# A transformer block on one Trainium2 core: layernorm tiles turned by DMA, and four smaller changes of order

## The chip, the cores and the metric

One core of a Trainium2 chip runs the whole kernel. The metric is the device time of one execution in microseconds (us). The engines are named as the profile names them: PE is TensorE's matrix products, PEld its weight loads, DVE is VectorE, ACT is ScalarE, POOL is GpSimd, and SP is SyncE, whose queue issues nearly all DMAs in program order.

## The reference

The input x has 2048 rows of 640 numbers in bf16. The block adds attention and then a gated product, each on a layernorm of what is there:

```python
x = A_x
h = x + _A_ref(_layernorm(x, axis=-1), A_wqkv, A_wo)      # 32 heads of 20, softmax over 2048 keys
h2 = h + _B_ref(_layernorm(h, axis=-1), B_w_gate, B_w_up, B_w_down)
# _B_ref: (x @ w_gate) * (x @ w_up) @ w_down, with 1728 inner columns
```

## The kernel before, in words

**Layout.** The 2048 rows are 16 tiles of 128, in four chunks of 512 (`QB`). Heads are packed four to a group (`HPG`), so there are eight groups (`NG`), each head in its slot of 32 partitions. Scores are made transposed (keys on partitions, 512 queries along the free side), so a *unit* is one tile of 128 keys by 512 scores of one head.

**The stream of units.** The exponentials are the body of the kernel. ACT takes most units, three or two banks at a time (line 727). DVE takes the rest with an integer trick: one operation per unit that writes int16 (line 739), and three per two units (lines 622, 624, 627). `on_dve` says how many units of a segment go to DVE (`D_CHUNK`, `D_WHOLE`, `D_HALF`), and those are the last ones of the segment's list, `units[cut:]`. Their due times lie between `EARLY` units before the segment's start and `LEAD` units before the end of ACT's part. PE makes the scores (line 719) and multiplies the exponentials with the values (line 857); the sums of the exponentials come out as an extra column.

**Segments and passes.** Pass 0 (the first 512 queries) goes chunk by chunk of keys for groups 0 to 3 (kinds "copy", "add", "last") and then whole for groups 4 to 7 (kind "only", 64 units each, 12 of them on DVE). Passes 1 to 3 are the other queries, partly cut in halves of 256.

**An order written out by a planner.** The Python code that builds the program keeps model clocks for PE, DVE and ACT (`clk`, `act_end`) and places every instruction by them. Each round `i` emits one exponential; the room left in the round, `limit_of`, with `EASE` or `HURRY` added, is filled with pieces of *jobs* from a queue: projections, transposes (`job_T`, `job_lnT`), output products, gated products. PE executes strictly in this order. If no job fits, `idle_products` adds products whose result is not used. `later(n, fn)` calls a function n rounds on.

**Layernorm.** DVE takes the statistics, POOL the inverse root, and DVE writes the normalized tile (`ln_apply`, line 240). For products over the 640 columns the tile must be turned: in `job_T` PE makes five transposes into a bank (line 320) and DVE copies them out (line 254). Layernorm 1 does this for four tiles per chunk into `lnT`; layernorm 2 does it in the tails, two tiles at a time, into `ln2T`. A turn may start 600 ns of model time after the tile is normalized (`ready`). The first four tiles (the head) and the last two (the end) are turned by code of their own.

**Keys and queries of most groups** go a longer way: a dense product (line 357), a copy to `dn`, a store to DRAM (line 365), and a read of it into the slots (line 388). The job's `READ` and `WRITE` are the model's times for this.

**Inverse sums.** When a segment closes, DVE copies its accumulator to SBUF (`asb_tile`; one wide buffer and two narrow). `norm` then sends the sums to DRAM and back (lines 757 and 758), POOL takes the inverse (line 761), it is stored (line 763) and read back spread over the partitions (line 766), and POOL multiplies (line 770). The two DMAs after POOL's inverse stand on SP's queue behind it.

**Tails.** When all groups of a set of rows are normalized, a tail is queued: output product with `wo`, residual, layernorm 2, turn, gated products (line 1174), down product (line 283) and store. The last tail (two tiles) comes after all units and has PE to itself. `wo` is loaded with four DMAs for each of eight groups (line 1039 clears the padding first); its tiles hold half of the query and key weights before that.

Of the kernel before, what the change touches and what calls it, by code (L numbers as in the profile page):

```python
# [18 lines left out]
P = 128  # L19
# [22 lines left out]
G1 = 4  # L42
GP = 4
D_CHUNK = (0, 0, 2, 2)
D_WHOLE = (12, 12, 12, 12)
D_HALF = (0, 6, 6, 6)
D_LAST = 4
SPLIT_1 = 4
# [19 lines left out]
SWITCH = 100  # L68
ROUND = 216
S_NS = SWITCH + ROUND  # L70
ACT_NS = {1: 478, 2: 904, 3: 1330}
RING = 2
EASE, HURRY = 100, 200
S_LAG = 270
AHEAD = 700
WAKE = 165
MINJOB = 600
AVLOW = 8
SLACK = 100
EB = (4, 3)  # L80
POOL_LN = 3500
WRITE, READ = 2500, 3500


@with_exitstack
def kernel(
# [39 lines left out]
    kb = const.tile([P, 1], F32, name="kb")  # L126
    qv = const.tile([P, 1], F32, name="qv")
    bad = const.tile([1, 1], I32, name="bad")
    wo = [const.tile([P, D], BF16, name=f"wo{g}") for g in range(NG)]
    NS = QB // SLOT  # L130
    seen_sums = const.tile([P, 2, NS], F32, name="seen_sums")

# [28 lines left out]
        nc.sync.dma_start(xs[0][:, t, :], x2d[t * P:(t + 1) * P, :])  # L161

    def wqk_half(c, hf):
        return (wo if hf else wqk)[c][:, 0:D].rearrange("p (m x) -> p m x", m=2)

    def load_wqk(hf):
        for c in range(KT):
# [157 lines left out]
        if given is None:  # L325
            ev(D // 2, held["slot"])

    def job_lnT(t):
        yield from job_T(lns[t], lnT[:, :, t * P:(t + 1) * P])

    def wslice(m, g, c):
        return wpad[c][:, m, HPG * g:HPG * (g + 1), :].rearrange("p h e -> p (h e)")
# [111 lines left out]
    for s, (p, g, lo, hi, _) in enumerate(segs):  # L444
        n = BANK // PASS[p][2]
        units = [(s, kt, j) for kt in range(lo, hi, n) for j in range(HPG)]
        cut = len(units) - on_dve(s)
        a0 = len(a_units)
        a_units += units[:cut]
        own = units[cut:]  # L450
        due += [a0 - EARLY + (cut - LEAD + EARLY) * (k + 0.5) / len(own) for k in range(len(own))]
        d_units += own
        left[s] = [n * (sum(u[2] == j for u in units) + sum(u[2] == j for u in own)) for j in range(HPG)]
# [296 lines left out]
    def norm(s, asb):  # L750
        p, g = segs[s][0:2]
        b, c0, w = PASS[p]
        n = w // 32
        rr = nrm.tile([P, 2, NS], F32, name="rr", bufs=3)
        r16, ri = rr[:, 0, 0:n], rr[:, 1, 0:n]
        sums = dram.tile([HPG, w], F32, name="sums", tag=f"sums{w}")
        nc.sync.dma_start(sums[:], asb[DH:P:SLOT, 0:w])
        nc.sync.dma_start(r16, sums[:].rearrange("j (c f) -> (j c) f", f=n))

        def back():  # L760
            nc.gpsimd.tensor_tensor(ri, r16, powers[:, 1:2].to_broadcast([P, n]), ALU.pow)  # L761
            scr = dram.tile([HPG, w], F32, name="scr", tag=f"scr{w}")
            nc.sync.dma_start(scr[:].rearrange("j (c f) -> (j c) f", f=n), ri)
            bc = nrm.tile([P, QB], F32, name="bc")
            for j in range(HPG):
                nc.sync.dma_start(bc[SLOT * j:SLOT * (j + 1), 0:w], scr[j:j + 1, :].to_broadcast([SLOT, w]))
            later(9, lambda: scale(bc))

        def scale(bc):
            nc.gpsimd.tensor_tensor(On[b % 2][g][:, c0:c0 + w], asb[:, 0:w], bc[:, 0:w], ALU.mult)  # L770
            note_sums(rr, n)
            later(4, lambda: done.add(("n", p, g)))
        later(8, back)

    def sums_to_rows(asb, w, ps=None):
        n = w // SLOT
        ps = bank() if ps is None else ps
        for t in range(w // P):
            nc.tensor.matmul(ps[:, HPG * t:HPG * (t + 1)], lhsT=asb[:, t * P:(t + 1) * P], rhs=late["if"][:, DH:P:SLOT], start=True, stop=True)
        mm(400, "turn")  # L780
        rr = nrm.tile([P, 2, NS], F32, name="rr", bufs=3)
        r16, ri = rr[:, 0, 0:n], rr[:, 1, 0:n]
        nc.vector.reciprocal(ri, ps[:, 0:n])
        bc = nrm.tile([P, QB], F32, name="bc")
        nc.vector.tensor_copy(bc[:, 0:w].rearrange("p (j e) -> p j e", e=SLOT), ri.rearrange("p (j e) -> p j e", e=1).to_broadcast([P, n, SLOT]))
        nc.vector.tensor_copy(r16, ps[:, 0:n])
        note_sums(rr, n)
        ev(w, held["slot"])
        return bc
# [72 lines left out]
            if sum(left[s]) == 0:  # L862
                close(s)

    sum_bufs = {"asb": -99, "ash0": -99, "ash1": -99}

    def asb_tile(w):
        tag = min(sum_bufs, key=lambda k: (sum_bufs[k], k)) if w == HW else "asb"
        sum_bufs[tag] = now["i"]
        return nrm.tile([P, QB if tag == "asb" else HW], F32, name=tag, bufs=1)  # L870

    def close(s):
        p, g, lo, hi, kind = segs[s]
        b, c0, w = PASS[p]
        if kind in ("copy", "only"):
            asb = parts[g] if kind == "copy" else asb_tile(w)
            if s == FINAL:
                nc.vector.tensor_copy(asb[:, 0:P], acc["t"][:, 0:P])
                nc.scalar.copy(asb[:, P:w], acc["t"][:, P:w])
            else:  # L880
                nc.vector.tensor_copy(asb[:, 0:w], acc["t"][:, 0:w])  # L881
            if kind == "copy":
                part[g] = asb
        else:
            asb = part[g]
            nc.vector.tensor_tensor(asb[:, 0:w], acc["t"][:, 0:w], asb[:, 0:w], ALU.add)
        dve_op(w / 0.96 + 75, clk["pe"] + 150)
        clk["acc"] = clk["dve"] + WAKE
        acc.update(seg=None, next=s + 1)
        acc["from"] = now["i"] + 2  # L890
        if s == FINAL:
            final["asb"] = asb
        elif (p, g) in FAST:
            urgent.append((("nf", p, g), job_norm(s, asb, clk["acc"]), None))
        elif kind in ("only", "last"):
            norm(s, asb)


# [62 lines left out]
    def gen_ln(ch):  # L961
        ts = range(ch * TPB, (ch + 1) * TPB)
        while hold(("x", ch)):
            yield WAIT
        mv = small.tile([P, TPB, 2], F32, name="mv")
        for k in range(TPB):
            bn(mv, k, xs[ch][:, k, :])
            yield 930
        for got in rstd_wait(mv, TPB):
            yield WAIT if got == WAIT else 0  # L970
        for k, t in enumerate(ts):
            apply1(t, *got, k)
            done.add(("a", t))
            ready["a", t] = max(clk["dve"], clk["pe"]) + 600
            yield 410

    def T_of(t):
        while hold(("a", t)):
            yield WAIT
        ensure_aux(("a", t))  # L980
        yield from job_lnT(t)

    def more_x(ch):
        load_x(ch)
# [50 lines left out]
    for t in range(NT):  # L1035
        value(t, 1)

    def load_wo(g):
        nc.gpsimd.memset(wo[g][:], 0.0)
        for j in range(HPG):  # L1040
            h = HPG * g + j
            nc.sync.dma_start(wo[g][SLOT * j:SLOT * j + DH, :], A_wo[DH * h:DH * h + DH, :])

    for b in range(1, NB):
        for t in range(KT):
            dense_job(0, t, b)
            if b == 1 and t + KT < NG:
                do(("wo", t + KT), lambda g=t + KT: load_wo(g))

    def spill(j):  # L1050
        src = dense[0][:, 0:QB].rearrange("(g j e) n -> j e g n", j=HPG, e=DH)
        nc.sync.dma_start(src[j, :, 0:G1, :], qa_all[SLOT * j:SLOT * j + DH, 0:G1, 0:QB])

    for g in range(KT):
        do(("wo", g), lambda g=g: load_wo(g))
        if g < HPG:
            do(("spill", g), lambda g=g: spill(g))


    late = {"res": {}}  # L1060
# [48 lines left out]
    def ln2_pieces(st, ts, key):  # L1109
        mv = small.tile([P, len(ts), 2], F32, name="mv")  # L1110
        for k, t in enumerate(ts):
            bn(mv, k, st["xr"][t][:])
            yield 930
        for got in rstd_wait(mv, len(ts)):
            yield WAIT if got == WAIT else 0
        for k, t in enumerate(ts):
            l_t = late["s"].tile([P, D], BF16, name="ln2")
            ln_apply(l_t[:], st["xr"][t][:], *got, k)
            st["l", t] = l_t
            done.add(("l2", key, t))  # L1120
            ready["l2", key, t] = max(clk["dve"], clk["pe"]) + 600
            yield 360

    def job_out(on, st, ts, key):
        pairs = [ts[k:k + 2] for k in range(0, len(ts), 2)]

        def T_pair(pair):
            for t in pair:
                while hold(("l2", key, t)) and end["pool"] is None and key is not None:
                    yield WAIT  # L1130
                ensure_aux(("l2", key, t))
                yield from job_T(st["l", t], st["ln2T"][:, :, t * P:(t + 1) * P])
        done.difference_update({("l2", key, t) for t in ts})
        while key is not None and hold(("xr",) + key):
            yield WAIT
# [252 lines left out]

    seen = {"t": 0, "last": False}
    i = 0  # L1390
    while pos["a"] < len(a_units) or pos["d"] < len(d_units):
        now["i"] = i
        emit_S(i)
# [37 lines left out]
    def general():  # L1431
        st = new_st(None)
        st["res"] = {}
        with tc.For_i(0, S, P) as r0:
# [1 line left out]
            load_tail(st, [0])  # L1436
            load_w(0, st)
            for g in range(NG):
                qs = nrm.tile([P, P], BF16, name="qs", tag="bc")
                nc.vector.memset(qs[:], BETA)  # L1440
                for j in range(HPG):
                    h = HPG * g + j
# [32 lines left out]
                ri = nrm.tile([P, HPG, 1], F32, name="ri", tag="rr", bufs=3)  # L1475
                ov = o[:, 0:P].rearrange("p (j e) -> p j e", e=SLOT)
                nc.vector.reciprocal(ri[:], ov[:, :, DH:VS])
                oq = nrm.tile([P, HPG, SLOT], BF16, name="oq", tag="asb", bufs=1)
                nc.vector.memset(oq[:], 0.0)
                nc.vector.tensor_tensor(oq[:, :, 0:DH], ov[:, :, 0:DH], ri[:].to_broadcast([P, HPG, DH]), ALU.mult)  # L1480
                ps = bank(BF16, P)
# [38 lines left out]
```

## Time and profile before

| | |
|---|---|
| median of three runs | 901.35 us (896.91 to 902.56) |
| the profiled execution | 899.62 us, span 897.8 us |
| PE, DVE, ACT, POOL busy | 92%, 78%, 90%, 22% of the span |
| granted PE clock, mean | 0.978 |
| DMA queue of SP | 95396 packets, 56.02 MB |

The profile page gives busy time by engine, the granted clock and the DMA share in 40 slices, the chain of work that ended last, and groups of instructions with the idle time before them. Other views of the same trace give single stretches, single tiles, and the order of instructions in time. A busy PE is not a PE at its peak, and idle time of an engine costs only where another waits for it.

### The profile page before, as it was taken

What the parts mean: (1) busy time and instruction counts of PE and PEld (TensorE: products, weight loads), DVE (VectorE), ACT (ScalarE), POOL (GpSimd) and SP (SyncE); (2) the same over time, 40 slices, a digit from 0 to 9 for tenths busy, and PEclk for the clock granted to TensorE, in tenths of its full rate; (3) what the DMA queues carried; (4) which work ended last, traced back from release to release, by engine and by line L of the source; (5) the groups of instructions that cost most, each with busy time, mean ns of one, the idle gap of its engine ahead of it and who ended that gap; (6) DMA issues with size and microseconds to landing.
All of it is one profiled execution on the core that took longest, in us unless ns stands there. A gap on an engine that the chain in (4) does not pass through costs nothing.

```text
span 897.8 us, 34224 instructions
## 1 busy us (share of the span) xinstructions
PE 830.1 (92%) x15185; PEld 406.0 (45%) x15185; DVE 704.3 (78%) x1384; ACT 804.0 (90%) x710; POOL 195.5 (22%) x258
## 2 busy tenths in 40 slices
PE   6899989998999999999899988999999999999996
PEld 4334333332334334445444545554553465445664
DVE  6665767996778989988888888988889888788631
ACT  6899997999999999999989999999999899999630
POOL 2110035123112321322312231223102412122100
PEclk8999999999999999999989999999999899899999
DMA  6111231342012232101314122322603010031310
GB/s 182 57 43 54 73 89 56 81 114 47 14 41 76 70 116 74 37 23 32 88 48 115 52 67 73 98 57 56 175 10 102 16 46 16 23 83 45 82 45 18
DMA packets 95550, 58.26 MB, mean 65 GB/s; under 512 B 24548, under 2 KB 93284, under 8 KB 95396
## 3 DMA queue, kind: packets, MB, share of 16 engines
q1 hardware_dynamic: 95396, 56.02, 23.1%
q8 instruction: 120, 1.97, 0.9%
q14 instruction: 34, 0.28, 0.1%
HBM read 47.60 MB, written 8.16 MB: 62 GB/s over the span
## 4 chain that ended last, share of the span: by engine, by line
PE 50%; DVE 23%; ACT 17%; issue 4%; DMA 3%; SPq 2%; POOL 0%; DVEq 0%; ACTq 0%; POOLq 0%
ACT E L727 17%; PE sc L719 12%; PE acc L857 10%; PE mi L1174 10%; PE mi L283 9%; DVE di L739 7%; DVE di L627 3%; DVE dm L622 2%; PE mi L357 2%; DVE dt L624 2%; PE f L1174 2%; DVE st L216 2%; PE f L283 1%; DVE hh L1206 1%; DVE u L254 1%
## 5 line engine op out<-in xcount | busy, mean ns | idle before, releaser
L727 ACT ACTIVATE E<-sc 128x1536 bf16<-128x1536 f32 (+1 forms) x679 | 786.7, 1263 | 43.9 <-PE mi L719 21.3
L739 DVE TENSOR_SCALAR di<-mi 128x512 int16<-128x512 f32 x350 | 238.0, 684 | 74.8 <-PE mi L719 71.6
L857 PE MATMUL acc<-E,vx 128*32 128x256 bf16 (+1 forms) x2532 | 224.4, 318 | 4.2 <-DVE asb L881 1.5
L719 PE MATMUL sc<-qa,kT 21*128 21x256 bf16 (+1 forms) x1800 | 206.2, 321 | 17.5 <-ACT E L727 14.4
L719 PEld LDWEIGHTS <-kT 21*128 21x128 bf16 x3072 | 85.6, 92 | 226.3 <-issue 215.1
L761 POOL TENSOR_TENSOR rr<-rr,powers 128x8 f32<-128x8 f32 (+1 forms) x44 | 98.7, 2243 | 304.7 <-DMA rr<-sums 291.8
L857 PEld LDWEIGHTS <-vx 128*32 128x32 bf16 x3612 | 82.3, 96 | 108.6 <-issue 98.2
L627 DVE TENSOR_TENSOR di<-di,dm 128x1024 bf16<-128x1024 bf16 x175 | 121.3, 693 | 4.1
L719 PE MATMUL mi<-qa,kT 21*128 21x256 bf16 (+1 forms) x376 | 99.0, 314 | 4.2 <-DMA kT<-dense 2.4
L622 DVE TENSOR_SCALAR dm<-di 128x1024 int16<-128x1024 int16 x175 | 79.7, 455 | 3.9
L857 PE MATMUL acc<-dt,vx 128*32 128x256 bf16 (+1 forms) x540 | 77.8, 313 | 2.8 <-DVE asb L881 2.0
L857 PE MATMUL acc<-di,vx 128*32 128x256 bf16 (+1 forms) x540 | 78.2, 313 | 0.7 <-DVE di L627 0.3
L624 DVE TENSOR_SCALAR dt<-di 128x1024 int16<-128x1024 int16 x175 | 77.8, 445 | 0.0
L719 PE MATMUL sc<-qb,kT 21*128 21x256 bf16 (+1 forms) x732 | 67.9, 294 | 4.7 <-ACT E L727 4.6
L283 PE MATMUL mi<-wd,hh 128*32 128x320 bf16 (+1 forms) x1432 | 67.2, 300 | 1.8 <-DVE hh L1206 0.7
L1174 PE MATMUL mi<-ln2T,wu 128*32 128x256 bf16 (+1 forms) x1210 | 58.8, 307 | 5.2 <-DVE di L739 2.5
L1174 PE MATMUL mi<-ln2T,wg 128*32 128x256 bf16 (+1 forms) x1210 | 54.7, 297 | 2.0 <-DVE di L739 0.8
L283 PEld LDWEIGHTS <-hh 128*32 128x32 bf16 (+1 forms) x1516 | 45.5, 96 | 20.3 <-issue 10.2
L1174 PEld LDWEIGHTS <-wu 128*32 128x32 bf16 (+1 forms) x1230 | 35.1, 99 | 19.9 <-issue 15.5
L283 PE MATMUL mi<-kT,ident 128*32 128x512 bf16 x608 | 43.2, 392 | 0.5 <-DVE dn L363 0.2
L1174 PEld LDWEIGHTS <-wg 128*32 128x32 bf16 (+1 forms) x1230 | 34.0, 96 | 13.6 <-issue 9.6
L1206 DVE TENSOR_TENSOR hh<-mi,u 128x512 bf16<-128x512 f32 (+1 forms) x48 | 31.7, 660 | 10.2 <-PE mi L1174 9.8
(135 smaller groups left out, 770.0 us busy)
## 6 DMA issues: line engine op xcount, KB each, us to landing
wu<-in_B_w_up_dram SPq DMA_DIRECT2D x30, 320.0 KB
wg<-in_B_w_gate_dram SPq DMA_DIRECT2D x30, 320.0 KB
dense<-dn SPq DMA_DIRECT2D x36, 128.0 KB
bc<-scr SPq DMA_DIRECT2D x64, 64.0 KB
bc<-scr SPq DMA_DIRECT2D x112, 32.0 KB
xr<-in_A_x_dram SPq DMA_DIRECT2D x16, 160.0 KB
out_dram<-xr SPq DMA_DIRECT2D x14, 160.0 KB
wd<-in_B_w_down_dram SPq DMA_DIRECT2D x13, 160.0 KB
```

Of the source, the lines that this page charges most:

```text
L216: nc.vector.bn_stats(st[:, h, :], halves[h] if halves else src[:, h * HALF:(h + 1) * HALF])
L283: nc.tensor.matmul(out[k:k + w, :], lhsT=lhsT[:, k:k + w], rhs=rhs, **flags)
L622: nc.vector.tensor_scalar(m16[:, 0:n], s16, M_MASK, M_BITS, ALU.bitwise_and, ALU.bitwise_or)
L624: nc.vector.tensor_scalar(t16[:, 0:n], s16, E_MASK, E_BITS, ALU.bitwise_and, ALU.bitwise_or)
L627: nc.vector.tensor_tensor(sb[:, 0:n], sb[:, 0:n], mb[:, 0:n], ALU.mult)
L719: nc.tensor.matmul(dst[:, h * w:(h + 1) * w], lhsT=kT[g][SLOT * j:SLOT * j + VS, (kt + h) * P:(kt + h + 1) * P], rhs=q_of(g, b, c0, w)[SLO ...
L727: nc.scalar.activation(e[:, 0:n], sc[:, 0:n], ACT.Exp, bias=EXP_BIAS, scale=SM_SCALE)
L739: nc.vector.tensor_scalar(t[:, k * BANK:(k + 1) * BANK], sd[:], EXP_A, 0.0, ALU.mult, ALU.max)
L761: nc.gpsimd.tensor_tensor(ri, r16, powers[:, 1:2].to_broadcast([P, n]), ALU.pow)
L857: nc.tensor.matmul(acc["t"][SLOT * j:SLOT * (j + 1), 0:w], lhsT=vx[kt][:, VS * h:VS * h + SLOT], rhs=e, start=(j not in acc["new"]), stop= ...
L1174: nc.tensor.matmul(ps[r0 + x:r0 + x + d, col:col + n], lhsT=wt[:, c, f0 + x:f0 + x + d], rhs=st["ln2T"][:, c, c0:c0 + n], start=(c == 0), ...
L1206: nc.vector.tensor_tensor(st["hh"][fp][:, f2:f2 + k, c0:c0 + n], g, u, ALU.mult)
```

## The change

- The turns of layernorm 1 for tiles 4 to 15, and of layernorm 2 for all tiles but the end's two, are five transposing DMAs each on SP, issued right after the tile is normalized (`turn`). Jobs may use the tile `TURN` = 6000 ns later by the model.
- In pass 0, groups 4 to 7, DVE takes the first keys of the segment instead of the last, and 14 units instead of 12.
- `norm` issues each hop in a later round than the one before it: read after 2, inverse after 4, store after 3, spreading read after 3, multiplication after 6. The "last" segments of groups 0 to 3 wait another `REST` + 6 g rounds first.
- Sums have two wide buffers and a narrow one, `bc` one wide and one narrow; the one that was taken longest ago is used.
- `wo` is one tile, cleared by POOL in spaced rounds and loaded with four DMAs.
- Model constants: `ACT_NS`, `EASE`, and DVE's clock at the start.

```diff
-D_WHOLE = (12, 12, 12, 12)
+D_WHOLE = (14, 12, 12, 12)
...
-ACT_NS = {1: 478, 2: 904, 3: 1330}
+ACT_NS = {1: 490, 2: 917, 3: 1343}
...
-EASE, HURRY = 100, 200
+EASE, HURRY = 50, 200
...
+REST = 30
...
+TURN = 6000
...
-    wo = [const.tile([P, D], BF16, name=f"wo{g}") for g in range(NG)]
+    wo_all = const.tile([P, NG, D], BF16, name="wo")
+    wo = [wo_all[:, g, :] for g in range(NG)]
...
-    def job_lnT(t):
-        yield from job_T(lns[t], lnT[:, :, t * P:(t + 1) * P])
+    def turn(dst, src, key):
+        for c in range(KT):
+            nc.sync.dma_start(dst[:, c, :], src[:, c * P:(c + 1) * P], transpose=True)
+        done.add(key)
+        ready[key] = max(clk["dve"], clk["pe"]) + TURN
...
         cut = len(units) - on_dve(s)
+        if p == "0" and g >= G1:
+            units = units[-cut:] + units[:-cut]
...
-        nc.sync.dma_start(r16, sums[:].rearrange("j (c f) -> (j c) f", f=n))
-
-        def back():
+
+        def read():
+            nc.sync.dma_start(r16, sums[:].rearrange("j (c f) -> (j c) f", f=n))
+            later(4, invert)
+
+        def invert():
             nc.gpsimd.tensor_tensor(ri, r16, powers[:, 1:2].to_broadcast([P, n]), ALU.pow)
+            later(3, write)
+
+        def write():
             scr = dram.tile([HPG, w], F32, name="scr", tag=f"scr{w}")
             nc.sync.dma_start(scr[:].rearrange("j (c f) -> (j c) f", f=n), ri)
-            bc = nrm.tile([P, QB], F32, name="bc")
+            later(3, lambda: spread(scr))
+
+        def spread(scr):
+            bc = bc_tile(w)
             for j in range(HPG):
                 nc.sync.dma_start(bc[SLOT * j:SLOT * (j + 1), 0:w], scr[j:j + 1, :].to_broadcast([SLOT, w]))
-            later(9, lambda: scale(bc))
+            later(6, lambda: scale(bc))
...
-        later(8, back)
+        later(2, read)
...
     def asb_tile(w):
-        tag = min(sum_bufs, key=lambda k: (sum_bufs[k], k)) if w == HW else "asb"
-        sum_bufs[tag] = now["i"]
-        return nrm.tile([P, QB if tag == "asb" else HW], F32, name=tag, bufs=1)
+        return oldest({"asb0": QB, "asb1": QB, "asb2": HW}, w)
+
+    def bc_tile(w):
+        return oldest({"bc0": QB, "bc1": HW}, w)
...
-        elif kind in ("only", "last"):
+        elif kind == "last":
+            later(REST + g * 6, lambda: norm(s, asb))
+        elif kind == "only":
             norm(s, asb)
...
             apply1(t, *got, k)
-            done.add(("a", t))
-            ready["a", t] = max(clk["dve"], clk["pe"]) + 600
+            turn(lnT[:, :, t * P:(t + 1) * P], lns[t], ("a", t))
...
         ensure_aux(("a", t))
-        yield from job_lnT(t)
...
+            for j in range(HPG):
+                nc.sync.dma_start(wo_all[SLOT * j:SLOT * j + DH, :, :], src[j])
...
             st["l", t] = l_t
-            done.add(("l2", key, t))
-            ready["l2", key, t] = max(clk["dve"], clk["pe"]) + 600
+            turn(st["ln2T"][:, :, t * P:(t + 1) * P], l_t, ("l2", key, t))
...
                 ensure_aux(("l2", key, t))
-                yield from job_T(st["l", t], st["ln2T"][:, :, t * P:(t + 1) * P])
...
     i = 0
+    clk["dve"] = max(clk["dve"], clk["pe"])
```

More of the change, by code (lines that the diff above doesn't have):

```diff
@@ L163, in wqk_half @@
     def wqk_half(c, hf):
-        return (wo if hf else wqk)[c][:, 0:D].rearrange("p (m x) -> p m x", m=2)
+        return (wo[c] if hf else wqk[c][:]).rearrange("p (m x) -> p m x", m=2)
     def load_wqk(hf):
@@ L783, in sums_to_rows @@
         nc.vector.reciprocal(ri, ps[:, 0:n])
-        bc = nrm.tile([P, QB], F32, name="bc")
+        bc = bc_tile(w)
         nc.vector.tensor_copy(bc[:, 0:w].rearrange("p (j e) -> p j e", e=SLOT), ri.rearrange("p (j e) -> p j e", e=1).to_broadcast([P, n, SLOT]))
@@ L863, in emit_AV, with oldest @@
                 close(s)
-    sum_bufs = {"asb": -99, "ash0": -99, "ash1": -99}
+    used_at = {}
+    def oldest(tags, w):
+        tag = min((k for k, n in tags.items() if n >= w), key=lambda k: (used_at.get(k, -99), k))
+        used_at[tag] = now["i"]
+        return nrm.tile([P, tags[tag]], F32, name=tag, bufs=1)
     def asb_tile(w):
-        tag = min(sum_bufs, key=lambda k: (sum_bufs[k], k)) if w == HW else "asb"
-        sum_bufs[tag] = now["i"]
-        return nrm.tile([P, QB if tag == "asb" else HW], F32, name=tag, bufs=1)
+        return oldest({"asb0": QB, "asb1": QB, "asb2": HW}, w)
+    def bc_tile(w):
+        return oldest({"bc0": QB, "bc1": HW}, w)
     def close(s):
@@ L1036, with clear_wo, load_wo, read @@
         value(t, 1)
[L1038 to L1042, printed above, removed]
+    def clear_wo(g):
+        nc.gpsimd.memset(wo[g], 0.0)
+    def load_wo():
+        for g in range(KT):
+            later(2 * g + 1, lambda g=g: clear_wo(g))
+        def read():
+            src = A_wo.rearrange("(g j e) n -> j e g n", j=HPG, e=DH)
+            for j in range(HPG):
+                nc.sync.dma_start(wo_all[SLOT * j:SLOT * j + DH, :, :], src[j])
+        later(2 * KT + 2, read)
+    for g in range(KT, NG):
+        later(9 * g, lambda g=g: clear_wo(g))
     for b in range(1, NB):
@@ L1046 @@
             dense_job(0, t, b)
-            if b == 1 and t + KT < NG:
-                do(("wo", t + KT), lambda g=t + KT: load_wo(g))
     def spill(j):
@@ L1052, in spill @@
         nc.sync.dma_start(src[j, :, 0:G1, :], qa_all[SLOT * j:SLOT * j + DH, 0:G1, 0:QB])
[L1054 to L1057, printed above, removed]
+    do(("wo",), load_wo)
+    for j in range(HPG):
+        do(("spill", j), lambda j=j: spill(j))
     late = {"res": {}}
@@ L1438, in general @@
             for g in range(NG):
-                qs = nrm.tile([P, P], BF16, name="qs", tag="bc")
+                qs = nrm.tile([P, P], BF16, name="qs", tag="bc0", bufs=1)
                 nc.vector.memset(qs[:], BETA)
@@ L1477, in general @@
                 nc.vector.reciprocal(ri[:], ov[:, :, DH:VS])
-                oq = nrm.tile([P, HPG, SLOT], BF16, name="oq", tag="asb", bufs=1)
+                oq = nrm.tile([P, HPG, SLOT], BF16, name="oq", tag="asb0", bufs=1)
                 nc.vector.memset(oq[:], 0.0)
```

## The prediction, written before the changed kernel ran

> **What bounds the kernel now.** I read the page first, then the stages, then the places where ScalarE (ACT) stops.
>
> ```profile
> span 897.8 us, 34224 instructions
> PE 830.1 (92%) x15185; PEld 406.0 (45%) x15185; DVE 704.3 (78%) x1384; ACT 804.0 (90%) x710; POOL 195.5 (22%) x258
> ```
> ```profile
> 28.00:125.00 97.00, 92.99 (x1339) 36.03 (x1340) 67.35 (x134) 94.43 (x84) 8.42 (x11) 1.00 0.20 60
> 125.00:150.00 25.00, 21.29 (x368) 9.55 (x360) 16.53 (x32) 18.17 (x16) 15.55 (x12) 0.93 0.20 55
> 150.00:270.00 120.00, 112.41 (x1421) 36.44 (x1417) 94.82 (x174) 116.69 (x103) 25.89 (x22) 0.99 0.24 61
> 270.00:846.00 576.00, 543.45 (x11439) 281.53 (x11439) 490.98 (x945) 547.78 (x472) 137.88 (x149) 0.98 0.25 65
> 846.00:898.00 52.00, 40.59 (x423) 30.92 (x411) 16.02 (x45) 9.16 (x18) 0.22 (x1) 0.94 0.10 28
> ```
> The columns of the second view are the stretch, its length, busy time of PE, PEld, DVE, ACT, POOL, then the granted clock. Until 846 us ACT's exponentials are the bound: ACT is busy 94.43 of 97 us, then 116.69 of 120, then 547.78 of 576. PE is nearly as full (543.45), but part of that is idle products which the scheduler puts in. The last 52 us are PE's own chain. So time is won before 846 us only by taking exponentials off ACT or by closing its gaps: 6.83 us in 125 to 150 and 28.22 us in 270 to 846; and at the end by giving PE less left-over work.
>
> ```profile
> 64.09 2.13 ACT E L727 x2
> ...
> 75.27 2.25 ACT E L727 x2
> ```
> In the chain that ended last, five pairs (3 + 2 units of 512 columns) lie between these two rows: 11.18 us for 25 units, so one unit is 0.447 us of a full ACT.
>
> ```profile
> 133.61 1.45 ACT L727 ACTIVATE E<-sc 128x1536 bf16<-128x1536 f32 x1 [2.13 <-PE sc L719]
> 135.74 1.02 ACT L727 ACTIVATE E<-sc 128x1024 bf16<-128x1024 f32 x1 [0.68 <-PE mi L719]
> 137.20 2.36 ACT L727 ACTIVATE E<-sc 128x1536 bf16<-128x1536 f32 x2 [0.44 <-PE sc L719]
> 146.97 3.33 ACT L727 ACTIVATE E<-sc 128x1024 bf16<-128x1024 f32 x3 [3.34 <-PE mi L719]
> ```
> ```profile
> 127.06 1.72 SPq L766 DMA_DIRECT2D bc<-scr  x4
> 128.82 1.52 SPq L388 DMA_DIRECT2D kT<-dense  x4
> 132.52 0.39 PE L719 MATMUL mi<-qa,kT 21*128 21x512 bf16 x1 [2.45 <-DMA kT<-dense]
> 143.22 2.35 PE mi L283 x60
> ```
> These are ACT's idle times in the worst stretch and what stands behind them. PE waited 2.45 us for the keys of the last chunk, which the read at L388 brings. It sat on SyncE's (SP's) queue behind the inverse-sum hop at L766. The waiter is a `mi` product: a DVE unit, and DVE's units of that segment were the *last* keys. That one wait gave ACT 2.13 + 0.68 + 0.44 = 3.25 us of idle, 1.33 us for each of PE's. The second gap, 3.34 us, stands behind a burst of value projections (L283 x60).
>
> **The change, part by part.** The sum is made against the profiled execution: 899.6 us, of which 897.8 are its span; the three runs have a median of 901.35, 1.7 above it.
>
> *First keys to DVE, the last norms put off.* From the fifth head group of pass 0 on, DVE takes keys 0 to 3 and ACT starts at the fourth, so chunk 3 is needed some 34 ACT units (34 x 0.447 = 15 us) later, and REST moves the four "last" norms 30 to 48 rounds back, out of SP's way. The first gap (3.25) goes; the second shrinks if PE is ahead by the turns it no longer makes (below). Bounds: 3 us if the burst stays, 6.8 if ACT gets full. I take **-6**, nearer to the upper end, because the stretches beside it have ACT at 97%.
>
> *14 units instead of 12 to DVE in four segments.* Eight units leave ACT: 8 x 0.447 = 3.6 us. What DVE gets:
>
> ```profile
> L739 DVE TENSOR_SCALAR di<-mi 128x512 int16<-128x512 f32 x350 | 238.0, 684 | 74.8 <-PE mi L719 71.6
> L627 DVE TENSOR_TENSOR di<-di,dm 128x1024 bf16<-128x1024 bf16 x175 | 121.3, 693 | 4.1
> L622 DVE TENSOR_SCALAR dm<-di 128x1024 int16<-128x1024 int16 x175 | 79.7, 455 | 3.9
> L624 DVE TENSOR_SCALAR dt<-di 128x1024 int16<-128x1024 int16 x175 | 77.8, 445 | 0.0
> ```
> A unit is 0.684 + (0.693 + 0.455 + 0.445)/2 = 1.48 us, eight are 11.8. DVE has 25 us idle in 150 to 270, so they are covered; without that cover a late unit holds a bank and PE behind it, and the 3.6 could turn into +2. I take **-3**.
>
> *Three sum buffers for one wide and two narrow.*
>
> ```profile
> DVE asb L881 <- POOL on L770: 2.4, 1, 2.4
> 200.00:250.00 50.00, 45.82 (x561) 14.76 (x558) 36.42 (x66) 47.95 (x44) 11.91 (x7) 0.97 0.15 36
> ```
> The one wide buffer made DVE, and PE behind it, wait 2.4 us for POOL; ACT lost 2.05 us in that stretch, which includes the usual. Two wide buffers end this. **-1.5** (0 to -2).
>
> *The turns.* 26 tiles (12 in layernorm 1, 14 in layernorm 2) no longer take five PE transposes, a DVE copy and two switches each; the head's four and the end's two stay.
>
> ```profile
> L320 PE MATMUL mi<-ident,ln 128*128 128x128 bf16 x70 | 6.9, 238 | 2.1 <-DVE di L739 1.7 <-DVE ln2T L254 0.2
> 448.00:458.00 10.00, 8.74 (x93) 3.69 (x92) 7.83 (x17) 7.13 (x7) 2.86 (x4) 0.67 0.07 16
> 538.00:546.00 8.00, 5.73 (x129) 3.71 (x127) 6.57 (x16) 6.43 (x7) 2.06 (x3) 1.00 0.07 19
> 622.00:630.00 8.00, 7.74 (x184) 4.58 (x180) 7.51 (x17) 7.96 (x8) 3.78 (x4) 1.00 0.11 21
> 709.00:718.00 9.00, 8.11 (x120) 3.99 (x119) 7.85 (x16) 5.96 (x6) 2.88 (x3) 0.62 0.02 3
> 807.00:815.00 8.00, 7.04 (x162) 4.16 (x158) 7.30 (x16) 7.48 (x8) 3.38 (x4) 1.00 0.08 15
> ```
> The PE time itself (about 0.5 us a tile) lies beside a busy ACT and is worth little. The waits around it are worth more: PE waits in order for the normalized tile, then for its copy. In the five stretches around a tail's turn ACT is idle 43 - 34.96 = 8.04 us; at the rate of the rest of 270 to 846 (20.2 us in 533) it would be 1.6. In two of the five the granted clock is 0.67 and 0.62. So up to 6.4 us lie there. With DMAs that are on time PE comes to the tile when it has long been turned. **-4.5** (0 to -6.4). Layernorm 1's turns fall where ACT is full, and are worth nothing but PE's lead into 125 to 150, counted above.
>
> *What the 130 new DMAs cost.* The trace has none of this kind. The nearest rows for an SP issue:
>
> ```profile
> 139.84 0.34 SPq L758 DMA_DIRECT2D rr<-sums  x1
> 12.98 4.12 SPq L196 DMA_DIRECT2D kT<-di  x7
> 811.89 2.99 SPq L766 DMA_DIRECT2D bc<-scr  x4
> 837.08 2.19 SPq L1091 DMA_DIRECT2D xr<-in_A_x_dram  x2
> ```
> That is 0.34, 0.59, 0.75 and 1.10 us for one. Call it d. From the last issue to the use took 132.52 - 130.34 = 2.2 us. A pair of tiles is ten DMAs and the schedule lets PE come about 6.4 us after the first tile is normalized (0.4 for the second, TURN 6.0): late by 10 d + 2.2 - 6.4, so on time up to d = 0.42. A 32 KB block in the queue's plain form is nearest to the 0.34 row; I take d = 0.4 and **0**. At the other end (1.1) each of seven pairs is 6.8 us late. In layernorm 1 twenty go at once, 8 us of SP at d = 0.4:
>
> ```profile
> 41.38 1.51 DVE L240 TENSOR_SCALAR xs<-xs,m,rstd 128x640 bf16<-128x640 bf16 x4
> 46.37 5.07 SPq L365 DMA_DIRECT2D dense<-dn  x3
> 53.11 1.44 SPq L388 DMA_DIRECT2D kT<-dense  x4
> 56.04 0.78 PE L320 MATMUL mi<-ident,xs 128*128 128x128 bf16 x10
> ```
> Chunk 2 is normalized from 41.4 and turned at 56.0, 14.6 us later, so its turns are hidden. But the stores of chunk 1's keys (46.4 to 51.4) and their read at 53.1 now stand behind up to twenty turns on SP, and ACT uses those keys within a few us: 0 to +5, I take **+0.5**, since PE stores them earlier too.
>
> The Trainium skill's "VectorE: DVE Perf Modes" (The three transpose paths) speaks against the change: it lists 390 ns for a 128x128 bf16 turn on TensorE and 1309 ns by DMA; ten in a row would by it be 13.1 us, an estimate from that page, and about 9 us late. Its "Advanced Engine Details and Errata" (X-Bar Transpose (TRN2)) has transposing DMAs as fast as plain ones, by which the zero stands. For TensorE this trace shows 238 ns a turn, and ten pipelined in 0.78 us, well under the first page; no run so far shows the DMA.
>
> *The end.* The turn in the last tail of the loop now comes 5.4 us later (TURN 6.0 for 0.6), and its gated products run up to the loop's end:
>
> ```profile
> 812.07 1.17 PE L1174 MATMUL mi<-ln2T,wu 128*32 128x256 bf16 x36 [0.64 <-DVE ln2T L254]
> 458.54 1.28 PE L1174 MATMUL mi<-ln2T,wg 128*32 128x256 bf16 x40
> 847.75 2.90 PE mi L283 x80
> ```
> They are 14 groups of 40 between 812 and 847, one per 2.5 us. 5.4 us less leaves 2.2 groups for after the loop at 1.28 us each, +2.8, less PE's own turns: **+2.5** (0 to +4). Other tails have pauses after them and absorb it.
>
> *At nothing:* the wo loads (4 DMAs for 32) and the spaced hops (22 rounds of waiting for 21, with SP free meanwhile) lie beside ACT's stream. EASE takes 50 ns from the room that PE's jobs have in a round and ACT_NS gives 13 back; DVE's starting clock moves which job goes where. The nearest number is ACT's idle time outside the turns, 20.2 us from 270 to 846: I take 0, and half of it as the bound either way.
>
> **Sum:** -6 - 3 - 1.5 - 4.5 + 0.5 + 2.5 = -12.0 from 899.6, **887.5 us**.
>
> **The rivals.**
> *Turns come late.* Place: the first product on ln2T after each pair. Above d = 0.42 PE, in order, stands, and the scores queued behind it stop ACT at 1.33 us for each us. At d = 0.75 (the L766 row) a pair is 3.3 us late: 7 x 3.3 x 1.33 = 31; chunks 2 and 3 need 15 + 2.2 of 14.6 us, 2 x 2.6 x 1.33 = 7; the 4.5 won at the turns is lost. 887.5 + 42.5 = **930**. It decides from d = 0.61, where the time passes 910. For it: twenty in a row are unlike anything in the trace; against it: SP's bare issue is 0.34 us. It is also the first page's rule.
> *SP's queue.* Turns hold up the keys of chunks 1 and 2, 5 us each less half of it for PE's lead, and tail loads: 887.5 + 5 + 4 = **896.5**. For it: 46.4 to 53.1 above; against: SP is idle before it.
> *It doesn't do what it says.* Value bursts keep the 3.34 us gap and DVE, at 14 units, gives the 3 back: 887.5 + 3.3 + 3 + 2 = **896**. For it: the burst is PE's work, not a wait; against: PE gives up some 6 us of turns before it.
> *More.* Without the slow clock after turns and with the smaller EASE, half of the 20 us idle outside the turns closes too: **877**. For it: PE's pauses and the low clock go together; against: ACT_NS gives jobs more room.
>
> **How the numbers follow.** Chances: forecast 0.52 (own range 880 to 894), late turns 0.14, SP's queue 0.13, not as said 0.11, more 0.10. A measurement here can tell about 1% (9 us) from no change, so faster means under 892.3 and slower over 910.4. Faster: 0.46 of the forecast's 0.52 and the 0.10, 0.56; slower: the late turns and 0.02 of SP's queue, 0.16; same 0.28, the rest. The range goes from 876 (more) to 908 (turns at d = 0.59) and leaves out the rest of the late turns.
>
> **What would show it.** Right: ACT busy 23 or more of 25 us in the stretch that holds the fifth group's start; ACT's instructions short by eight units; no DVE copies to lnT and ln2T but the head's and end's; ACT within 4% of full around the turns; PE's first product on ln2T not waiting for a DMA; a transposing DMA under 0.45 us on SP. Wrong: PE waiting for "DMA ln2T" or "DMA lnT" by microseconds, a low clock after it, or SP occupied over 10 us by one chunk's turns.

## The result, and the profile after

The change makes the kernel slower: 1000.31 us median (998.0 to 1003.01, four runs) against 899.13 us (895.39 to 902.56, four runs) on the same chip, a ratio of 1.1127 [1.1063, 1.1191]. The forecast was 887.5 us, with a range up to 908.

The page of the changed kernel: the span, the engines, the granted clock in 40 slices, the shares of the chain of waits, and ACT's exponentials.

```profile
span 996.2 us, 34444 instructions
PE 866.2 (87%) x15223; PEld 405.8 (41%) x15223; DVE 703.4 (71%) x1378; ACT 802.2 (81%) x707; POOL 190.1 (19%) x258
PEclk9875799999999979999979997999698979998998
PE 41%; DVE 21%; ACT 17%; SPq 10%; issue 5%; DMA 4%; POOL 1%; DVEq 0%; POOLq 0%; ACTq 0%
L735 ACT ACTIVATE E<-sc 128x1536 bf16<-128x1536 f32 (+1 forms) x676 | 784.9, 1258 | 143.1 <-PE sc L727 90.4
```

No engine has more work than before: ACT is busy for 802.2 us (804.0 before), DVE for 703.4 (704.3). The 98 us are idle time, and the chain has an entry that hardly counted before: SP's queue, 10% of the span (2% before). PE's 866.2 us, 36 more than before, come with nearly as many products (15223 after 15185): where the clock digit falls to 5 or 7, each one takes longer.

The stages of the changed kernel, in the columns that the prediction explains:

```profile
28.00:125.00 97.00, 55.40 (x651) 17.63 (x647) 29.93 (x66) 44.36 (x39) 6.95 (x13) 0.72 0.18 44
125.00:150.00 25.00, 24.11 (x342) 8.44 (x334) 15.44 (x27) 24.68 (x23) 0.00 (x0) 1.00 0.23 68
150.00:270.00 120.00, 113.20 (x1560) 38.33 (x1560) 106.38 (x196) 114.77 (x100) 29.53 (x21) 1.00 0.28 70
270.00:846.00 576.00, 522.62 (x9956) 245.75 (x9952) 442.40 (x844) 505.18 (x437) 128.03 (x134) 0.93 0.24 62
846.00:998.00 152.00, 130.53 (x2511) 83.17 (x2503) 92.66 (x196) 95.15 (x91) 18.05 (x26) 0.95 0.18 47
```

The first row has layernorm 1: ACT is busy 44.36 of 97 us where it had 94.43, at a clock of 0.72. In 270 to 846, where the tails with layernorm 2 are, ACT has 505.18 where it had 547.78. The last row still holds work of the loop, whose last exponential ends at 943.4 us instead of 846.35. Between them nothing is lost.

The changed kernel's transposing DMAs on SP by tile (min/median/max ns that each holds the queue, first and last start, count):

```profile
L333 SPq DMA_TRANSPOSE lnT<-xs x60: 1102/1230/1965, 31.2 to 117.7; - x60
L333 SPq DMA_TRANSPOSE ln2T<-ln x70: 1093/1230/1992, 335.2 to 912.8; - x70
```

One turning DMA holds SP for 1.23 us. The prediction had 0.4, between bounds of 0.34 and 1.10. SP's queue in order of time (start, length, what, count), and then ACT's long pauses (in brackets, with what ended them):

```profile
31.23 25.98 SPq L333 DMA_TRANSPOSE lnT<-xs  x20
57.31 0.53 SPq L371 DMA_DIRECT2D dense<-dn  x1
61.49 20.26 SPq L333 DMA_TRANSPOSE lnT<-xs  x15
82.48 6.19 SPq L333 DMA_TRANSPOSE lnT<-xs  x5
88.77 1.00 SPq L371 DMA_DIRECT2D dense<-dn  x2
91.29 1.44 SPq L394 DMA_DIRECT2D kT<-dense  x4
92.83 26.11 SPq L333 DMA_TRANSPOSE lnT<-xs  x20
...
352.37 12.56 SPq L333 DMA_TRANSPOSE ln2T<-ln  x10
```
```profile
58.40 1.02 ACT L735 ACTIVATE E<-sc 128x1024 bf16<-128x1024 f32 x1 [16.46 <-PE sc L727]
94.97 1.45 ACT L735 ACTIVATE E<-sc 128x1536 bf16<-128x1536 f32 x1 [20.20 <-PE sc L727]
120.11 1.02 ACT L735 ACTIVATE E<-sc 128x1024 bf16<-128x1024 f32 x1 [8.64 <-PE sc L727]
...
366.14 1.02 ACT L735 ACTIVATE E<-sc 128x1024 bf16<-128x1024 f32 x1 [9.05 <-PE mi L727]
```

Read side by side: each chunk of layernorm 1 holds SP for some 26 us, and ACT's long pauses come in or just behind these, 16.46 + 20.20 + 8.64 = 45.3 us. The stores of keys (L371) wait behind the turns as well: the first starts at 57.31, behind twenty of them. The keys of chunk 1 are copied for their stores by 68.1 us, but the last of these starts at 88.77, behind chunk 2's turns, and the read (L394) at 91.29; PE starts on these keys at 93.49, and ACT's pause of 20.20 us ends at 94.97. A pair of tiles in a tail holds SP for 12.56 us, and ACT's pause of 9.05 us ends just behind it. What PE did in that tail, and its waits over the whole kernel (us, times, longest):

```profile
361.03 0.62 PE L1202 MATMUL mi<-ln2T,wu 128*32 128x512 bf16 x4 [5.30 <-DMA ln2T<-ln]
362.33 0.62 PE L1202 MATMUL mi<-ln2T,wu 128*32 128x512 bf16 x4 [0.68 <-issue]
...
364.88 0.62 PE L1202 MATMUL mi<-ln2T,wu 128*32 128x512 bf16 x4 [0.65 <-DMA ln2T<-ln]
```
```profile
PE mi L1202 <- DMA ln2T<-ln: 33.2, 25, 5.3
PE mi L363 <- DMA lnT<-xs: 19.7, 7, 11.4
PE mi L286 <- DMA lnT<-xs: 15.0, 4, 13.1
PE sc L727 <- DMA kT<-dense: 5.6, 1, 5.6
```

The four groups of products start 1.26 to 1.30 us apart: the tile arrives by fifths, one turning DMA each, and PE follows SP's beat. PE stood 33.2 us for the tiles of layernorm 2, 34.7 us for those of layernorm 1, and 5.6 us for the keys of chunk 1.

### The profile page after: what moved, and what is told of

Read it like the earlier page. It is cut to its first block, busy times and chain, and to the rows that moved or that the text cites. A ratio compares the mean times of both kernels' runs of the same rounds, so it can differ in the third digit from the quotient of the medians.

```text
span 996.2 us, 34444 instructions
## 1 busy us (share of the span) xinstructions
PE 866.2 (87%) x15223; PEld 405.8 (41%) x15223; DVE 703.4 (71%) x1378; ACT 802.2 (81%) x707; POOL 190.1 (19%) x258
## 4 chain that ended last, share of the span: by engine, by line
PE 41%; DVE 21%; ACT 17%; SPq 10%; issue 5%; DMA 4%; POOL 1%; DVEq 0%; POOLq 0%; ACTq 0%
ACT E L735 17%; PE mi L1202 10%; PE sc L727 10%; SPq L333 9%; PE acc L874 8%; DVE di L747 7%; PE mi L286 6%; DVE di L635 3%; DVE dm L630 2%; PE mi L363 2%; DVE dt L632 2%; DMA ln2T<-ln 2%; PE f L286 2%; PE f L1202 2%; DVE st L219 2%
## 5 line engine op out<-in xcount | busy, mean ns | idle before, releaser
L747 DVE TENSOR_SCALAR di<-mi 128x512 int16<-128x512 f32 x358 | 243.3, 685 | 94.2 <-PE mi L727 89.1
L874 PE MATMUL acc<-E,vx 128*32 128x256 bf16 (+1 forms) x2524 | 230.9, 323 | 7.6 <-DVE asb L904 5.2
L635 DVE TENSOR_TENSOR di<-di,dm 128x1024 bf16<-128x1024 bf16 x179 | 126.6, 707 | 4.1
L1202 PE MATMUL mi<-ln2T,wu 128*32 128x256 bf16 (+1 forms) x1170 | 65.5, 324 | 36.5 <-DMA ln2T<-ln 33.2
L727 PE MATMUL sc<-qb,kT 21*128 21x256 bf16 (+1 forms) x732 | 71.3, 305 | 3.3 <-ACT E L735 2.4
L286 PE MATMUL mi<-wd,hh 128*32 128x320 bf16 x1344 | 62.4, 300 | 0.7 <-DVE di L747 0.4
L1202 PE MATMUL mi<-ln2T,wg 128*32 128x256 bf16 (+1 forms) x1170 | 58.7, 317 | 0.4
L369 DVE CAST dn<-mi 128x512 bf16<-128x512 f32 x36 | 24.7, 686 | 48.2 <-PE mi L363 47.1
L286 PE MATMUL mi<-kT,ident 128*32 128x512 bf16 x732 | 53.3, 390 | 2.1 <-DVE di L747 2.0
L363 PE MATMUL mi<-lnT,wqk 128*32 128x512 bf16 x320 | 35.3, 453 | 20.5 <-DMA lnT<-xs 19.7
```

What stands on the lines that cost most here:

```text
L286: nc.tensor.matmul(out[k:k + w, :], lhsT=lhsT[:, k:k + w], rhs=rhs, **flags)
L363: nc.tensor.matmul(ps[k:k + SLOT, :], lhsT=wqk_half(c, col // HALF)[:, m, col % HALF:col % HALF + SLOT], rhs=lnT[:, c, ch * QB:(ch + 1) * ...
L635: nc.vector.tensor_tensor(sb[:, 0:n], sb[:, 0:n], mb[:, 0:n], ALU.mult)
L727: nc.tensor.matmul(dst[:, h * w:(h + 1) * w], lhsT=kT[g][SLOT * j:SLOT * j + VS, (kt + h) * P:(kt + h + 1) * P], rhs=q_of(g, b, c0, w)[SLO ...
L747: nc.vector.tensor_scalar(t[:, k * BANK:(k + 1) * BANK], sd[:], EXP_A, 0.0, ALU.mult, ALU.max)
L874: nc.tensor.matmul(acc["t"][SLOT * j:SLOT * (j + 1), 0:w], lhsT=vx[kt][:, VS * h:VS * h + SLOT], rhs=e, start=(j not in acc["new"]), stop= ...
```

## The experiments

The ratios are to runs of the kernel before on the same chip. Its median moved from 899 to 904 us from one set of runs to another, so ratios are compared rather than microseconds. One hundredth is about 9 us.

### 1. Whose loss is it: the turns back on PE, one layer at a time, and the turns alone

*All else of the change, with all 26 tiles turned by PE* (both places that call `turn`, and the jobs that used its tiles):

```diff
-            turn(lnT[:, :, t * P:(t + 1) * P], lns[t], ("a", t))
+            done.add(("a", t))
+            ready["a", t] = max(clk["dve"], clk["pe"]) + 600
...
+        yield from job_T(lns[t], lnT[:, :, t * P:(t + 1) * P])
```

> The changed kernel with all 26 turns back on TensorE; its other edits stay. Theory A (the whole loss is the turning DMAs, each of which holds SP's queue for 1.23 us and comes late to PE): what is left of the change is worth what the prediction gave its other parts, -6 - 3 - 1.5, so about 889 us (882 to 896) and 111 us under the changed kernel. Rival B (the other edits, 14 units on DVE, later hops, EASE, cost part of the 100 us): over 905 us.

892.03 us (889.33 to 899.48, ten runs), 0.9916 [0.9878, 0.9953].

*The kernel before, with only the turns by DMA and `TURN` = 6000*:

```diff
+            turn(lnT[:, :, t * P:(t + 1) * P], lns[t], ("a", t))
...
+            turn(st["ln2T"][:, :, t * P:(t + 1) * P], l_t, ("l2", key, t))
```

> The kernel before with only the turns moved to transposing DMAs, TURN 6000. Theory A: all of the loss and none of the other gains, 1000 to 1015 us. Rival B: under 980 us, since a part of the loss needs the other edits.

1013.95 us, 1.1245 [1.1189, 1.1302].

*The changed kernel with layernorm 1 alone back on PE, so that layernorm 2's 70 DMAs stay* (the edit of the first kernel above, at `lnT` only):

> The changed kernel with layernorm 1's turns on TensorE and layernorm 2's 14 tiles by DMA. Theory A: the first run's time plus what ACT's long gaps in the tails of the changed kernel sum to (9.0, 5.7, 10.2, 8.3, 2.5, 2.1, 5.9, 1.6, 1.7, 7.4: 54 us), about 943 us (930 to 955). Rival C (the tails' loss is a consequence of the lost order in layernorm 1, and the tails alone would be in time): under 915 us.

949.8 us, 1.0554 [1.0511, 1.0598].

*The changed kernel with layernorm 2 alone back on PE, so that layernorm 1's 60 DMAs stay* (at `ln2T` only):

> The changed kernel with layernorm 2's turns on TensorE and layernorm 1's 12 tiles by DMA. Theory A: the first run's time plus ACT's three long gaps of the first 125 us (16.5, 20.2 and 8.6: 45 us), about 934 us (922 to 945), and with the run before it the two parts add up to the whole. Rival C: over 960 us, most of the loss.

938.9 us, 1.0443 [1.0376, 1.051].

The turns are all of the loss, and the rest of the change is a small gain. Above the 0.9916 of all turns on PE, layernorm 2's cost 0.0638 (57 us) and layernorm 1's 0.0527 (47 us), together 0.1165; the whole change stands 0.1211 above it. So the two add up within the intervals, and neither hides behind the other. How much of layernorm 1's part is late tiles and how much late keys, no run separates.

### 2. What a turning DMA is paid by: the number, or the bytes

*Each DMA cut in two of 64 rows, 260 instead of 130 for the same bytes:*

```diff
-            nc.sync.dma_start(dst[:, c, :], src[:, c * P:(c + 1) * P], transpose=True)
+            for r in range(0, P, P // 2):
+                nc.sync.dma_start(dst[:, c, r:r + P // 2], src[r:r + P // 2, c * P:(c + 1) * P], transpose=True)
```

> The changed kernel with every transposing DMA cut in two of 64 rows: 260 DMAs, same bytes. Price per DMA (the run with one DMA a tile says so): each still holds SP's queue for about 1.2 us, 322 us in all, and the time passes 1090 us. Price per byte beyond some size: 0.6 us each, about 1000 us.

1177.05 us in one run. *One DMA for a whole tile of 128 x 640, 26 for the same bytes:*

```diff
-        for c in range(KT):
-            nc.sync.dma_start(dst[:, c, :], src[:, c * P:(c + 1) * P], transpose=True)
+        nc.sync.dma_start(dst, src[:, 0:D], transpose=True)
```

> The changed kernel with one transposing DMA for a tile of 128 x 640 instead of five of 128 x 128: 26 instead of 130, same bytes. If the 1.23 us on SP is a price per DMA: one takes 1.3 us, a pair is ready 5 us after the first tile, 885 to 895 us. If it is a price per byte: one takes 4.7 to 6.2 us, a pair is still 5 to 8 us late, 960 to 1000 us.

893.22 us (889.86 to 898.03, ten runs), 0.9901 [0.9864, 0.9937]. The same view by tile, of the halves and then of the whole tiles, the latter with SP's queue in order of time:

```profile
L334 SPq DMA_TRANSPOSE lnT<-xs x120: 1088/1226/2050, 31.7 to 194.0; - x120
L334 SPq DMA_TRANSPOSE ln2T<-ln x140: 1088/1226/2430, 420.6 to 1090.0; - x140
```
```profile
L332 SPq DMA_TRANSPOSE lnT<-xs x12: 1201/1232/1737, 31.8 to 60.3; - x12
L332 SPq DMA_TRANSPOSE ln2T<-ln x14: 1204/1242/1762, 288.2 to 805.5; - x14
```
```profile
31.76 5.85 SPq L332 DMA_TRANSPOSE lnT<-xs  x4
...
288.16 2.56 SPq L332 DMA_TRANSPOSE ln2T<-ln  x2
```

1.226 us for 64 x 128, 1.230 for 128 x 128, 1.232 and 1.242 for 128 x 640: the price is that of one DMA, and its size does not matter here. A chunk's turns hold SP for 5.85 us instead of 25.98, and a pair's for 2.56 instead of 12.56. Cutting in two added 130 DMAs and 177 us, 1.36 us for each; joining five into one took away 104 DMAs and the whole loss. The stages with whole tiles:

```profile
28.00:125.00 97.00, 93.28 (x1371) 34.42 (x1371) 66.64 (x132) 94.25 (x83) 6.97 (x13) 1.00 0.37 84
125.00:150.00 25.00, 24.58 (x394) 9.57 (x387) 20.65 (x40) 24.99 (x23) 0.00 (x0) 1.00 0.05 14
150.00:270.00 120.00, 108.41 (x1367) 34.44 (x1367) 105.81 (x185) 112.39 (x98) 42.31 (x32) 1.00 0.32 77
270.00:846.00 576.00, 551.68 (x11605) 283.03 (x11603) 482.82 (x933) 542.87 (x469) 132.62 (x150) 0.99 0.27 66
```

ACT has 94.25 of the first 97 us again, at clock 1.00. This is the best version that ran, about 1% better than the kernel before; from the changed kernel with PE's turns (0.9916) its interval doesn't part it.

### 3. Would it have done to tell the planner that the tile is late?

*Layernorm 2 by five DMAs a tile, layernorm 1 on PE, and the due time from a model of SP's queue:*

```diff
-        ready[key] = max(clk["dve"], clk["pe"]) + TURN
+        sp["free"] = max(sp["free"], clk["dve"], clk["pe"]) + KT * 1260
+        ready[key] = sp["free"] + 2500
```

> Layernorm 2 by DMA, layernorm 1 on TensorE (the third run's kernel), but a turned tile is due by a model of SP's queue, 5 x 1.26 us per tile one after the other and 2.5 us to land, instead of 6 us. Theory A1 (the tails lost 58 us because PE's order was written for an earlier date, so PE stood; the DMAs themselves do no harm): PE waits no more, 895 to 910 us, the rest being gated products that come some 10 us later and run on past the loop's end. Theory A2 (the queue is blocked for loads and hops as well): over 925 us.

935.42 us, 1.0381 [1.0327, 1.0436]. It took a quarter of layernorm 2's loss away (1.0554 before, 16 us). Its last exponentials, the stretch behind them, SP, and the chain there:

```profile
839.53 5.00 ACT L738 ACTIVATE E<-sc 128x1536 bf16<-128x1536 f32 x4
```
```profile
844.00:935.00 91.00, 60.64 (x996) 47.84 (x995) 29.00 (x68) 9.28 (x18) 2.29 (x7) 0.87 0.24 65
```
```profile
856.07 12.58 SPq L335 DMA_TRANSPOSE ln2T<-ln  x10
```
```profile
866.16 1.23 SPq L335
867.43 2.33 DMA ln2T<-ln
869.80 3.63 PE mi L1207 x64
```

The loop ends at 844.5 us, as with PE's turns (844.7), and ACT is idle before its exponentials for 47.4 us in all, as with PE's turns (47.0; 97.5 with the fixed due time). Only two long stops are left, of 4.60 and 4.90 us. But 91 us follow instead of 53. The last tail now comes behind the loop as a whole: a read of its input on the chain from 843.4 us, its layernorm, its turns at 856, and its products. Both expectations had a part: PE hardly waits inside the loop any more, but the time is that of the rival, over 925 us. With five DMAs a tile the queue's 12.6 us a pair can be paid inside the loop as stops or behind it as a longer end.

### 4. Does a shorter due time help once a tile is one DMA?

```diff
-TURN = 6000
+TURN = 3000
```

(on the kernel with one DMA a tile)

> One transposing DMA a tile, TURN 3000 instead of 6000. A pair needs 0.4 + 2 x 1.25 + 2.3 us from the first normalized tile, 5.2, and PE comes after 3.4 plus what the pieces of a round add. If the queue alone decides: late by up to 1.8 us, seven pairs, 0 to 10 us slower than with 6000. If the late gated products at the end decide: 1 to 3 us faster, about 0.988 of the kernel before.

902.95 us, 1.0021 [0.9994, 1.0049]: worse than with 6000, 0.9901. PE waits for a turn again, 4.2 us in all:

```profile
PE mi L1201 <- DMA ln2T<-ln: 4.2, 3, 2.4
```

These 4.2 us, and 1.4 more for layernorm 1, are half of the 11 us. In the two profiles the difference lies in the loop, whose last exponential ends at 846.7 us instead of 838.7; behind it follow 52.5 and 52.8 us. What makes the other half isn't shown.

### 5. The other parts

*One DMA a tile alone, on the kernel before, `TURN` = 6000:*

```diff
+        nc.sync.dma_start(dst, src[:, 0:D], transpose=True)
```

> The kernel before with only the turns moved, one transposing DMA a tile, TURN 6000. The prediction's terms for the turns alone, -4.5 + 2.5 + 0.5, give 1.5 us faster, ratio 0.998 (0.992 to 1.003); if the turns on TensorE were what held the tails back, 0.99; if DMAs on SP's queue hurt even when there are few, over 1.005.

902.29 us, 1.0021 [0.9989, 1.0053]: turned on time, the turns by themselves win nothing. The last exponentials, of the kernel before and then of this one (span 899.2):

```profile
839.06 7.29 ACT L727 ACTIVATE E<-sc 128x1024 bf16<-128x1024 f32 x6
```
```profile
838.35 3.86 ACT L730 ACTIVATE E<-sc 128x1536 bf16<-128x1536 f32 x3 [0.18 <-PE mi L722]
```

The loop ends at 842.2 instead of 846.35, 4.1 us earlier, and 57.0 us follow instead of 51.4, 5.6 us more. What the loop gains goes to the end. Nor is it gained at the tails:

```profile
125.00:150.00 25.00, 22.71 (x361) 8.96 (x357) 22.95 (x39) 23.25 (x21) 16.31 (x14) 1.00 0.24 63
270.00:846.00 576.00, 540.01 (x11342) 276.34 (x11335) 478.70 (x915) 538.71 (x466) 131.81 (x148) 0.99 0.26 65
```

Between 125 and 150 us ACT has 23.25 us instead of 18.17. From 270 us to the loop's end, where the tails are, it is idle for 33.5 us (572.2 - 538.7) instead of 28.2.

*All turns on PE, with 12 units to DVE in the four segments instead of 14:*

```diff
-D_WHOLE = (14, 12, 12, 12)
+D_WHOLE = (12, 12, 12, 12)
```

> The kernel with all turns on TensorE (the first run) and 12 units instead of 14 on DVE in groups 4 to 7 of pass 0. The first run's profile has DVE busy 43.55 of 50 us from 200 to 250 and PE waiting there for DVE. Theory D (the eight units only moved the bound from ACT to DVE): the same as the first run or faster, 887 to 892 us. Theory P (the prediction's -3): 3 us slower than the first run, 895.

898.79 us, 0.9979 [0.9949, 1.001], against 0.9916 with 14: the eight units are worth about 0.6%, 5.7 us; the two intervals just touch.

*All turns on PE, with the last keys to DVE as before:*

```diff
-        if p == "0" and g >= G1:
-            units = units[-cut:] + units[:-cut]
```

> The first run's kernel, but DVE takes the last keys of groups 4 to 7 again. Theory P (the keys' order closes the gap at 130 us, worth 6): 897 to 900 us and ACT idle several us again between 125 and 150. Rival (the put-off norms and free queue do it, not the order): 892 us, no gap there.

896.02 us, 0.9942 [0.9908, 0.9977] against 0.9916 [0.9878, 0.9953]: 2.3 us, and the intervals overlap. With the last keys to DVE, the stretch from 125 us and the next one, and ACT's pause in the first; below them, with the first keys, the same stretches:

```profile
125.00:150.00 25.00, 23.11 (x422) 10.79 (x414) 19.88 (x39) 20.84 (x19) 0.00 (x0) 1.00 0.05 15
150.00:270.00 120.00, 110.37 (x1341) 33.42 (x1333) 104.66 (x186) 112.11 (x98) 41.40 (x31) 0.97 0.30 75
```
```profile
144.04 7.07 ACT L733 ACTIVATE E<-sc 128x1024 bf16<-128x1024 f32 x6 [4.08 <-PE mi L725]
```
```profile
125.00:150.00 25.00, 24.71 (x431) 10.50 (x424) 22.14 (x45) 25.00 (x23) 0.00 (x0) 1.00 0.03 8
150.00:270.00 120.00, 110.00 (x1288) 33.69 (x1280) 102.23 (x183) 108.05 (x94) 41.55 (x31) 0.93 0.32 79
```

With the first keys ACT is full in 125 to 150 (25.00 of 25 against 20.84), as predicted. In the stretch behind it has 108.05 against 112.11: 4.16 us won and 4.06 given back by 270 us. DVE's load doesn't explain that: of the 50 us from 200 it is busy for 43.55 with the first keys and 44.85 with the last (36.42 in the kernel before). The execution profiled with the first keys was the longest of its ten, 899.48 us against a median of 892.03, so what it gave back, at a clock of 0.93, may be its own.

*One DMA a tile, `TURN` = 3000, 13 units in the four segments:*

```diff
-D_WHOLE = (14, 12, 12, 12)
+D_WHOLE = (13, 12, 12, 12)
```

> The run with one DMA a tile and TURN 3000, but 13 units on DVE in groups 4 to 7 of pass 0. DVE is full there with 14 and ACT lost some 11 us from 150 to 225; four units come back to ACT (1.8 us). If DVE is over its limit: 1 to 4 us faster than with 14. If ACT's count decides: 2 us slower, as 12 units were slower than 14.

897.68 us, 0.9964 [0.9939, 0.9989], against 1.0021 with 14: here fewer units are better, by 0.6%, where with PE's turns 14 beat 12 by as much. The sum of what DVE takes off ACT is thus not what decides at this size. Every edit also changes where the planner puts all later jobs, and effects of half a per cent can't be told from that by these runs.

## Why the prediction was wrong

**The step that failed** is "What the 130 new DMAs cost", and in it one term: d, taken as 0.4 us. It measured 1.23, above the upper bound of 1.10 too, because both bounds came from plain DMAs (the nearest row for a block in the queue's plain form was 0.34 us), and a turning one is another operation for the queue. The mechanism was in the text as "Turns come late", with the point from which it decides, d = 0.61. With d = 1.23 in the prediction's own formulas a pair is 12.3 + 2.2 - 6.4 = 8.1 us late, seven pairs 7 x 8.1 x 1.33 = 75 us; chunks 2 and 3 are 24.6 + 2.2 - 14.6 = 12.2 us late each, 32 us; with the lost 4.5 that makes 887.5 + 112 = 1000 us against 1000.31. That the sum agrees so closely is luck: above the kernel with all turns on PE, layernorm 2 measured 57 us where the formula has 75, and layernorm 1 47 where it has 32. The formula's 2.2 us from the last issue to the use was too long as well: a turned tile lands 1.1 us after its hold (shown in the chain of experiment 3), which takes 7 x 1.1 x 1.33 = 10 us off the 75.

**"Its turns are hidden"** for layernorm 1 failed by the same term: 14.6 us of cover against 26 us of queue. The formula also left out chunk 1, whose turns from 31.23 to 57.21 stand ahead of ACT's 16.46 us of pause. In the kernel before it is normalized from 26.26 and turned at 37.70, 11.4 us of cover, so the formula would have it 24.6 + 2.2 - 11.4 = 15.4 us late, 20 us more.

**The keys behind the turns** were taken as +0.5, between 0 and +5, and this failed too. The last of their stores came 20 us late (copied by 68.1, stored from 88.77), and it is these keys that ended ACT's longest pause, 20.20 us, after PE had waited 11.4 us for the tile and 5.6 us more for them (with one DMA a tile PE waits 1.1 us for keys). So the rival "SP's queue" came together with the late turns, and from the same d.

**Whose rule held.** The Trainium skill's "VectorE: DVE Perf Modes" (The three transpose paths) has 1309 ns for a 128 x 128 turn by DMA; the trace shows 1230 ns of queue, and the estimate of 13.1 us for ten that the prediction made from it stands beside 12.56 measured. The prediction gave that case 0.14, with SP's bare 0.34 us against it, and set the page's TensorE figure aside with this trace's rows; its figure for the DMA held. The Trainium skill's "Advanced Engine Details and Errata" (X-Bar Transpose (TRN2)), with turns as fast as plain DMAs, isn't borne out for the hold of the issuing queue: 1.23 us against 0.34. But the 1.23 us are the price of one DMA and not of a block of 128 x 128, as the 128 x 640 row shows.

**1.33 us of ACT for one of PE's wait** lies between the two rates measured: 45.3 us of ACT's pauses for 34.7 + 5.6 of PE's waits in layernorm 1 (1.1), and 57 us of time for the 36.8 that PE waited in the run with layernorm 2 alone by five DMAs (1.6). A part of what exceeds the wait is that the products behind it run slowly: 0.62 us for four, at a granted clock of 0.50, where the same group took 0.40 at a clock of 1.00.

**The other terms**, without the turns, were to give -6 - 3 - 1.5 = -10.5 us and gave 0.84%, 7.6 us. First keys: -6 predicted, about -2.3 measured, with intervals that overlap; the pause was closed as described, and why so little came of it isn't shown. Units: -3 predicted, -5.7 measured with PE's turns, and of the other sign in the kernel with `TURN` = 3000, so their size stays open. The sum buffers, and the parts put "at nothing", were not tried alone. The turns, when on time: -4.5 at the tails predicted; the loop did end 4.1 us earlier, but by the pause at 125 us, while ACT's idle time from 270 us on grew, so the agreement of the number is chance. The end: +2.5 predicted and +5.6 measured. With d at its predicted worth the time would probably have been near the 893 us of the kernel with one DMA a tile, inside the forecast's own range, but not by the terms as they stood.

**Still open:** why a shorter due time costs 11 us with one DMA a tile, when only 5.6 us of PE's waits go with it; why the first keys win so little; and what the units are worth under each order of jobs.

## What to carry to other kernels

An operation that the trace doesn't have can't be bounded by rows of another kind on the same queue: the 0.34 to 1.10 us of plain DMAs said nothing of the turning one, and a case that turns on such a price deserves a range that reaches to where the rival leads. On a queue that is paid by the DMA, first ask for the widest instruction: the same 26 turns cost 11% of the kernel as 130 DMAs and nothing that these runs can tell as 26. A due time given to a planner must count the whole queue behind which the last piece stands; here that moved most of the cost rather than removing it. And what is issued after a long run of DMAs waits as well: ask which stores and reads will stand behind it.

## What the runs showed of the hardware

- A transposing DMA held the issuing queue for 1.23 to 1.24 us (median), whatever its size from 64 x 128 to 128 x 640 bf16; plain ones held it for 0.34 to 1.10 us in the rows of the kernel before. In the chain of experiment 3 the tenth turn is issued from 867.43 to 868.65 and lands at 869.76: 2.33 us after its issue began, 1.1 after its hold ended.
- During and after PE waits of 13.1 and 11.4 us the granted clock was 0.50. The two stretches of the changed kernel:

```profile
44.80:61.90 17.10, 6.61 (x49) 1.50 (x49) 2.24 (x5) 2.47 (x2) 0.00 (x0) 0.50 0.24 62
75.50:102.80 27.30, 11.17 (x77) 2.53 (x77) 2.08 (x3) 4.95 (x4) 0.00 (x0) 0.50 0.19 45
```

PE was at work in 17.8 of these 44.4 us, all of them at half the clock.
